# Reciprocal deviations: one pass per group on two tensor operands, or scalar passes per tile, with a new order of issue

## The chip, the cores and the metric

The kernel runs on one core of a Trainium2 chip. The metric is the device time of one execution in microseconds (us); where several executions are told of together, it is their median. The profile and the trace are of one profiled execution of the kernel before.

The engines have short names here. PE multiplies matrices, and PEld is its weight load. DVE works on vectors, ACT applies functions, POOL is a second, slower vector engine, and SP issues the transfers between the memory of the core and the chip's main memory. Each engine takes its instructions in order and waits for the others by semaphores.

## The reference

The input is one array x of 2048 rows and 512 columns. Two kinds of layer alternate, four in all, each fed with a layer norm of x and added back to x:

```python
def _layernorm(x, axis=-1, eps=1e-5):
    m = jnp.mean(x, axis=axis, keepdims=True)
    v = jnp.var(x, axis=axis, keepdims=True)
    return (x - m) / jnp.sqrt(v + eps)
...
X = jnp.fft.rfft2(x) * (w_r + 1j * w_i); y = jnp.fft.irfft2(X)      # A
y = einsum((x @ w_gate) * (x @ w_up), w_down)                       # B, inner width 1792
...
x = x + A(layernorm(x)); x = x + B(layernorm(x))
x = x + A(layernorm(x)); x = x + B(layernorm(x))
```

What matters for the change is the division by the deviation, sqrt(v + eps), once per row and layer.

## The kernel before, in words

x stays in the core as xs, 16 tiles of 128 rows and 512 columns. A spectral layer takes each tile through a forward transform (fwd, line 452, results E), then 16 middle steps that multiply by the filter (middles, tiles fs, dp, zp, vq), then an inverse transform per tile (inv, tiles yi and yo), whose result is added to xs. All transforms are matrix products on PE. The feed-forward follows in blocks of 128 of the 1792 inner columns: up products (gx, gy, gw, gz, gv) from the normalised input, kept as xA and xS, with weights wt; then down products (db, or ex, ey, ez, ev, ew), added to xs by DVE. The products are split in a high and a low part each, and fewer products than the plain count are made by sums beforehand, so that ACT and POOL are busy with rounding, differences and sums.

Layer norm runs tile by tile. `stats` (line 396) puts mean and variance of a tile into mv, by DVE (bn_stats, bn_aggr) or by two passes of ACT (sq) and two small tensor_scalar of DVE. `rstd` (line 412) then works on a group of tiles that share mv and the four-row tile rs. ACT makes a first value of 1/sqrt(v + eps), r, and r²/2. DVE refines it: row 1 is (v + eps) · r²/2; row 2 is (row 1 - 1.5) · r, the negated refined value; for the inverse side, row 3 is -mean · row 2. Each of these is one `scalar_tensor_tensor` over all tiles of the group, with two operands in the core's memory and one constant. Groups hold two tiles, but for the first four forward tiles, which are groups of one. There are 18 forward groups with two passes and 16 inverse ones with three: 84 passes.

Who reads rs: on the forward side, ACT multiplies the tile's transform matrix (tw or tws) by row 2 before PE may use it (fwd_rest, line 459). On the inverse side, `normed` (line 428) lets ACT make xn from xs with row 2 as factor and row 3 as offset; PE then transposes xn into tq (first eight tiles of a layer, build_x), or DVE transposes it and it goes through main memory (last eight, stage_x).

The order of the work is fixed beforehand. The kernel first lists 4811 steps, each with its engine and with what it reads and writes, by keys such as (rs, 2); `Plan.op` (line 231) makes of these which step needs which. ORDER, a packed string, holds the order in which the steps are issued; every engine gets its own in that order. PLACES holds, for each tile that is first used, which buffer of its ring it takes. Both strings were worked out ahead from estimates of each step's time, and the kernel only reads them (`Plan.order`, line 258). In this order, the first eight inverse transforms of a layer precede the feed-forward; the last eight are woven into its first half.

Of the kernel before, what the change touches and what calls it, by code (L numbers as in the profile page):

```python
# [28 lines left out]
def consts():  # L29
# [91 lines left out]
    'CQT5`mje7G9&*SD2dVCFXH)k{30Z8XaKe0qBI%O$i`JswVQmLRiQL44^IBZ{-Uu<xYvO8@;L589YFbgpr8neE+TP^pfm1cs)n-&JbRnPN<IhIQJ`O}u8{6~4c2&)>*Fj2tJkG%cqaCh&ad+Z'
    '$RwQy@-kTE9nRxU{4)*V8T1xxVn1eF=Ln1~MtAu-_rm&<DFgCNq}72o1?#v8#lc#HyW4z$YvZ@Kndc&O*C+Hl!&%I)XfJwKs5-qvUxA+#tW%tC;C@vc%$r#3ybX>+(CSUT=EO#?<18Ay8~yw'
    'Pn}`9Y&2T=IyI|L|{5**+_Ng7M62AeRmZDkKY-@~Kqfj7rl1|^KR*mksmN#=pT$hFQCQv(Az(QCW^N-lE6;*^5S7Kz-px0HVZ=ugWdB4u?3-2qWx-vAA-%zQ>V;#}`E`ES6<4G5se~4Xc1Y+'
    'H2x19##ybbnkNn`j)j9kXz86{0LHKt{*2_4|?Xf@`ofkzp7pT_Zr^bqz5&`10&#xLN9X*8ZRgiln(%<{VXc8bOMd~g#+Ii?Q3taqzmpJbub)aOI|lt!scYRJoR?<L4hcsj=eT)b_{qNAel-h'
    '5chPFN=M=8(<#&%(b#_#k+#O<z(WT{V<?;`>)<-0@MYQ6B3aKwN2v>pHM1kw`fb4fLg@JOdQ<hPT&(%_eah#EXWML633>^tc345J_&KA9yOi5B(YV-q-vB&FAN67T>1LxU<a_HL<R${Q-7W5'
    '$k@!FXQ_&3g@o)ja9ugB#BR3RhEXBrqEDWj)%KLcnbaFB;tz3&T=WkY*>8e4B}=s)*9^U8hLgK*Q_!*iU=gDmIRmbBrj-rR-ZTI-}zU_r5K`5d1I-t*Uz>y?{gCGqFt_t`OUk_wXLN}n0pE_'
    ';1q|O{x~1v?&7<S&2lj&+uaY(jW)7k67KeMeeAuxg|=I+EY6FY<1z#L7N$IxN0(eKML{aUV+g$fZjVxBUd9C!!FQmiFjE4)yPVo%&8hI_1ZoBUji&>yw@KmFyaQ1<k8hajE|o(ONt<G&tFDY'
    'G3y(7Nr|Q<wgAyGBc?AW$z?)&M@?F4^cPs@!<7wo*Oit&j%=D%i0om3=UfYhS7{d7&lddv5;WA<82lzcsC9#IT-Ew?aMYJ2m&r-honLC>EJk(nNzC)oG$!NK*KV2a4wj0=Q2dwBiRxe?;@gQ'
    '1@vB}nezg?iA66LrIjI2x9?m8&0s8r5}<yhp?KaexJ!}hx1>Kvl@%kcl>T$7ud#T<_BOysCB&ev%<6GBa>J2YLC=BhW<5E+;oJkz~l?pME0!`&E;FsJd`g3?@q`4<r`fViHB)o!^})JUm5&k'
    '`m5b?YHF%G`duBxpSgxdrCj<v9Ax6*IZ+6(jL;51--+e1%$K#AW2t%J7BV$TGcQAC8y8FSoc3W~TejOoL3sD%Noae7D2u4PA-}ASdrY1p6KNR1TxEtcJA`$=6*ZZQwFN8Y+T<A6YVTTRhpy$'  # L130
    '&f;VX%7zT(_;67dCW~S3n8}>@Jo-=I04Zt9$Dj0=wcmgxjr4n>^R6>a;MP<cNtkV4biGTY%&EIUUprJnLFX_+u`A2(PeOVgxg>w;x|z*I>XgTWWCn?Ne{Tc&2Ny7$4Q`PIY&az2e=je!tc93'
    'VI>3kluPE`v=XuJ6Ht2r7W5@#)xvEHgt|;_>&O=HIZpLrY!xbvHLe(u#73__Eir{9CwU$1T-d<@isTyZgb7zPRmA0*SheeXc(k9Zj`Cx;UIY63&_#C{vDg8(CE>{ic(sg>tUlL^h9}pe@3}9'
    'y@w~C7oSSIJ^2i`clX0n>i#3xG$u4?=!1nT8$oD7HAM4NakgbfYRT<X1mydh3Y&mz;NRHdj&jjO8I#9+p@X`>B2zSNkFXLlA$>oLI(^llX7kW-ZR^MZWyM100yMv3m89dU~pw*_THyg5OX7e'
    'C(nYmAGvlYGX9kRYxXJCg9v7ZN@8SeQuQVg^f)3eX5cyp)!iG8cMhI;s?o@AE}_G8e;h~<JY|3qe-scYl|?dEumZ3>PRUUhoK&cPVT&D*^%0*728tY{@hJ_jm3^{$yHH{TX0$0M=MUB2Xfr;'
    '<+RulTB0ipZv6bT2Dtx)YG!YxX*S<CU}%sW;CKnVf&aE8tsZWyni+=i7zIF9(1H1|oLN@(R&Z@bH4y!aCUVX>X%V@_N_|MN+$Aak5K_?(DdcX2W*yQ}Ob_9OJS$-@J+aGR;pR{qD}Q!@Wy9)'
    'TVMjpnw4NqtiUi8)ip(V&B!3#!tXUsCvL4FAU#(ZEfU#qv)nMqS|(ro$|P|?%W;pJ*yFRl2?*iAQEo$-m-Dfw^Rxu@c@oq-uJd0u=yC<l-lEYJKCfxij_5nWt`&)o~$v~o@0@H0#y#Vo!{E~'
    ')h^;XW{cO~Bm${j<13IrFPt61s`>EQOcwNR=?$;DnPtj)b79X-y{~LnShYk}KVDd9SaNFuHSjLk5XFc_Ei#Or1lHS&oLog?PMjkB`G{CzDdKf!g0XO%B9@9;4fz@SVT@P@dC1+1kVhCIx`8}'
    'DBted~aDP0HpxN$Un#|WIU@9T@^u_99_$2j&UkL>bS+dppI2KcX@H8F>qBG)nyhgar;G&z#D1aTxXvHG9r+}W|A7QVHVD-IudJwq{;$*7I12_%7<!LQbktS-M9p^I4a^#MF?urqdv78@AZ1('
    'vQR5=P2iy_JHm1rzI&GYFgE`Us=RtnH6pyz3zS}e;TOT0-vfawMO$C$Z5yK{iHEPbo~)dw;egtOy_q+fDX%(%pBsV`99EPh>Wst+&4A=<bIbUFYTE*cfdVmuiPTb?Vv%Qq>JKcJVe)=$&{zF'
    '7n_Z@Y9e3-Y{)yC-=fW;_Qgk5#*$EU^SUcT=sEVyQt-(t4H(X)^D`-FAG8jn<~=IJR&qu6wCurE&-$>%`Io$VH@{hhs77lW^*w5_+0<;?8W09Lu|*mo6F|ccIdW#QKep{jTu0p!Xl8r4xzwG'  # L140
    '~&_Fp4hmc{zdc-kD`Gr6>vTHtoWw*P%OpqSoM*SSUU&vC4R?a#0*}AI`VBA3XSKxfEms&@I0*!rSja1yzwxJk7l@7GmfQlS`VETK<newUPBNY+M*(Cpf$oHyiGY3iy8+?JQnZVg#E+{y91#{'
    'gL*+nrQvOkw;(%*DD~Np@N^^kdIY)f2F8V|r0eoAt%g0G4C^R~)!5Ym3fTe#wT+9Y+`>uLN2QCk93OVpBxnwjYG61h6|LsEaH?g*zT3dt#;62F&}4U$-qQ#&5jzjlTzrCui>L6%kW^>2TU75'
    'Z(X4jWjMRdA+*mVGNB4s~m*Q--VmP7lEOx1`I91SVSEX(<tR#T?AqQGaMjf}0&$$w&17_^gZbLNr`Q}IV^_ZpiM1wb2WS_>8VQxVppP4*2n6udiJxb!2prnrQ<^)_7VCFIQbI(w$bri^Gpk|'
    '3Ns*{O443)WGgQe-XF1n-SEQu~Hsl1D%k4+VLQ$TG`qH;@JPc-#QP>+t2fQI(-QF;wH(9Z{T6=}x1qox)0q9qu$2gf@u6*4~z9Y|bXq*d$*puz3z_h_ufdy9Q?V9Nu5+iECZC$+Y}3W?Qpr;'
    'zb(8L_UXU787nwgT!of-m2tquwRRTX5hzG>zY*8QjUmBJxI{R+Ron6f#Lo`WR0HxvXQOU7l+2aSuC&X`Zi7Q7+2}M%>B5>s>BE3Ch)0#99jp6w>InRVDv0u*wxKrCpJHFWX4{ebh^^A|sLMB'
    'bbqfs=vMZ|NW>(Lm>;tCWtVtRt_?<w`T1C<RiO^m)F9R3a~*#kAcfoKvzaH>^|>pYcz_);%+Y-J+Q(G#Evt31pfFv{O<sMLm*v0x18k7-WHx=!-8m}0`7#+JKl8bBd%EB!u>3jx}f9>TA9jk'
    'KgjlgM1DvoPIHiWUN+*ONLh4qN-aowYgK^q<jxD8=;Jyl+z89aP+p5DrZZF>JJhAp-e2}#<lYFSMfy1LS}C;m&e(9oX9m74Ks6olUlx1_*|vd~Y7@w>62u#-P#td*cDV$cTpT_!(+<g-V(SB'
    'g<syqb2;@EAG;kIgszTCJN(D-(?_J>Q_8`Y#h34KqTNASnawqSG4G(I=!nZVEm>j-NSG|8wvBG*y1y>4{K`!4zsD=cg1|Z|YhzTWCkMTAg)nRvDhgzZxYKNQP<OXbmvEMn+)B?C6U+s|LA=m'
    'jHcar~@|1zOYGXEVu4NV_l|9)}$8Trg;fAoHQYQgqW5KjV>h%>42>j5`3SLy|MN{4hWqQmoag}*^QzYib5n<;!A$Zj*g201jRc^H+5o$kOB?}LTs0OMRY?Vap%m<6RwhDY5{ja^f3P35-1>V'
    '6V3>@c2$t9SWp5|lL^wpt^IyF<Zuw)Prs@GYQ|+S-p5X_e4BCs?q^B5tX@w<=ii8c=vHo}_C(?ZM!9iPGVqp{`2gEG%LLsv4vAnGQeN0K1o7U<_6}p<Uq$peqS+A{iBqbdkdp1N!o96}0<<L'  # L150
    '5a`S@2SB))?k_wy#G`1S2A8BjlE}p|7&V5L;8>9^+`5j=^l85<n`*>JvqP=;iom#Yb7?#K~*WevHd)OhQedkDkYr}Av+<$WFf<ThT|OUW(6d%3w6#Z4ru1_<MDRLWG`xh)f#z6m|d<Lo~_58'
    '9z3uGIF462|Dqgh)zv2hiAjv^NoS}%ed>AuYxM+jiB#)fhPg{1?MV39GM)kidB6?9Gt`#Av-^RL(qJ{)So*+=K}iOzIEBXp%Sn&jV!p(lFCguCRGZfT^Cj~V)nyNj7jtQXdU_^MOT6|{S0W0'
    'D1}XsGJON}=6r80X_DVF0QcbQ#_6kEhs6o3a(+S^CDw4H`H7mqI%@kz(;-)57q704I=c%Gnvlu%c1qR)$*ijI@X!KPcs}+o)57i%+&}+2RbpaKlc}&ng*K@aESK{8M5H$S>Y&nhNOs@7>C2A'
    'Yw58n=}0w*(%hpoS;SyA#ry2kcw?VBd(%KnP+u$Pgvky5cvWz!6?)A4bZyK-%)IS^YFBPe|lAE%e0%Z3zZzST}`3U5~oo9_CP>^~WGbyXwCL)Jg*;!GpV?nZw=j%P3<&NSph(9}3^=l3XDYd'
    '8B-@|?u$Xk^JskTej}f836zx8PNd3tYG<i})i5`U%7jU`$#8c}@bxu1lv-w^(|eXXD$0{!2sS8SE(r$Z?`O*63ds*Q;S`o1N&Onpy6mDbi%S4n```9j=1OP%NAed4@s;*A%g};IecWzd!IY8'
    'tx*D#Mk0lGsP&K^MTeb>RDNE_p^48L%~D9oMVaP@}2K4BPXuacOcRs>%^Z^cRsI`f>iZUT#tT{N|3X)|LVC7>aEQ|&7;6TkF((M0=H4I)l;ZyjCy=7Z^MeB=k@UHv%re&Fe+Vb(r6VP&6!%o'
# [1011 lines left out]
```

## Time and profile before

| what | value |
|---|---|
| median of 3 runs | 1048.07 us (1047.96 to 1051.95) |
| profiled execution | 1046.97 us |
| its span, first to last instruction | 1045.2 us |
| mean granted PE clock | 0.999 |
| busy, DVE / ACT / POOL | 799.7 / 419.4 / 747.8 us |
| main memory traffic | 193.66 MB, 185 GB/s on average |

A row of a group or of the order of time names the engine, the operation, the tiles as out<-in, and shapes as partitions x elements. In rows in order of time, the first number is the start and the second the duration, both in us, and a bracket gives the time that the engine had stood idle and what released it. In a row of a stretch, the numbers after the length are busy time and count for each engine, then the PE clock, the share of the transfer engines and GB/s. All helpers record under line 304 of the kernel, so rows are told apart by their tiles.

The table of stretches, in us from the span's start: forward transforms of the first layer up to about 28, the middle steps to 71, first inverse transforms to about 100, the first feed-forward to 525, in whose second half the forward transforms of the next layer are woven, the last forward transforms to 548, middle steps to 590, inverse transforms to 625, and the second feed-forward to the end.

### The profile page before, as it was taken

What the parts mean: (1) busy time and instruction counts of PE and PEld (TensorE: products, weight loads), DVE (VectorE), ACT (ScalarE), POOL (GpSimd) and SP (SyncE); (2) the same over time, 40 slices, a digit from 0 to 9 for tenths busy, and PEclk for the clock granted to TensorE, in tenths of its full rate; (3) what the DMA queues carried; (4) which work ended last, traced back from release to release, by engine and by line L of the source; (5) the groups of instructions that cost most, each with busy time, mean ns of one, the idle gap of its engine ahead of it and who ended that gap; (6) DMA issues with size and microseconds to landing.
All of it is one profiled execution on the core that took longest, in us unless ns stands there. A gap on an engine that the chain in (4) does not pass through costs nothing.

```text
span 1045.2 us, 18605 instructions
## 1 busy us (share of the span) xinstructions
PE 1023.6 (98%) x6544; PEld 878.4 (84%) x6544; DVE 799.7 (77%) x1457; ACT 419.4 (40%) x989; POOL 747.8 (72%) x950
## 2 busy tenths in 40 slices
PE   8998999999999999999999999999999999999998
PEld 6777987888888888889987779888888888888897
DVE  8779778768866677777878796788897766777778
ACT  6678534423432422232276693322343411222221
POOL 6978999999998665666698467555679954456571
PEclk9999999999999999999999999999999999999999
DMA  9613476586694864665282006446786265565532
GB/s 359 277 66 122 123 261 225 181 276 219 190 293 165 284 212 131 220 209 187 76 302 95 10 3 207 157 140 236 212 254 203 99 216 199 196 217 184 199 122 82
DMA packets 129469, 193.66 MB, mean 185 GB/s; under 512 B 39264, under 2 KB 50784, under 8 KB 127328
## 3 DMA queue, kind: packets, MB, share of 16 engines
q1 hardware_dynamic: 129232, 192.21, 54.3%
q8 instruction: 52, 0.85, 0.3%
q14 instruction: 41, 0.34, 0.1%
q10 hardware_dynamic: 144, 0.26, 0.1%
HBM read 145.52 MB, written 46.92 MB: 184 GB/s over the span
## 4 chain that ended last, share of the span: by engine, by line
PE 89%; DVE 6%; ACT 2%; DMA 2%; issue 1%; DVEq 0%; SPq 0%; ACTq 0%
PE gz L304 15%; PE gx L304 14%; PE db L304 7%; PE gv L304 7%; PE gw L304 7%; PE gy L304 7%; PE ez L304 5%; PE ex L304 5%; PE ev L304 3%; PE zp L304 3%; PE dp L304 3%; PE vq L304 3%; PE ew L304 3%; PE ey L304 2%; DVE xs L304 2%; PE yi L304 2%
## 5 line engine op out<-in xcount | busy, mean ns | idle before, releaser
L304 PE MATMUL gx<-xA,wt 128*128 128x512 f32 (+1 forms) x756 | 175.3, 367 | 1.6 <-DMA wt<-gu 1.6
L304 PEld LDWEIGHTS gx<-xA,wt 128*128 128x128 f32 x756 | 130.6, 189 | 23.6 <-DMA wt<-gu 1.8
L304 POOL TENSOR_TENSOR sf<-q,sf 128x256 fp32r<-128x256 f32 x92 | 68.2, 744 | 78.5 <-ACT sf L304 71.4
L304 POOL TENSOR_TENSOR sf<-cc,sf 128x256 fp32r<-128x256 f32 x96 | 71.3, 745 | 54.9 <-ACT sf L304 54.2
L304 DVE TENSOR_TENSOR xs<-xs,db 128x512 f32<-128x512 f32 x128 | 85.3, 682 | 24.3 <-PE db L304 23.7
L304 PE MATMUL db<-wd,h 128*128 128x512 f32 x336 | 90.6, 392 | 0.7 <-DVE xs L304 0.6
L304 PE MATMUL gz<-xS,wt 128*128 128x512 f32 (+1 forms) x378 | 88.4, 369 | 1.2 <-DVE q L304 1.1
L304 PE MATMUL gy<-xS,wt 128*128 128x512 f32 (+1 forms) x378 | 88.3, 369 | 0.2
L304 PE MATMUL gz<-xA,wt 128*128 128x512 f32 (+1 forms) x378 | 88.1, 368 | 0.0
L304 PE MATMUL gw<-xS,wt 128*128 128x512 f32 (+1 forms) x378 | 87.8, 367 | 0.0
L304 PE MATMUL gv<-xS,wt 128*128 128x512 f32 (+1 forms) x378 | 87.5, 367 | 0.0
L304 PEld LDWEIGHTS gv<-xS,wt 128*128 128x128 f32 x378 | 65.5, 189 | 11.2 <-POOL xS L304 0.2
L304 PEld LDWEIGHTS gz<-xS,wt 128*128 128x128 f32 x378 | 64.5, 189 | 12.0 <-DVE q L304 1.9
L304 ACT COPY s<-gx 128x512 f32<-128x512 f32 (+1 forms) x63 | 33.9, 538 | 101.1 <-PE gx L304 97.5
L304 PEld LDWEIGHTS gw<-xS,wt 128*128 128x128 f32 x378 | 65.2, 189 | 10.9
L304 PEld LDWEIGHTS db<-wd,h 128*128 128x128 f32 x336 | 62.1, 188 | 14.6 <-DVE xs L304 1.7
L304 PEld LDWEIGHTS gy<-xS,wt 128*128 128x128 f32 x378 | 64.5, 189 | 11.2 <-DVE q L304 0.8
L304 PEld LDWEIGHTS gz<-xA,wt 128*128 128x128 f32 x378 | 64.8, 189 | 10.5
L304 ACT CAST sf<-q 128x256 fp32r<-128x256 f32 x92 | 37.1, 406 | 77.8 <-DVE q L304 41.7
L304 DVE TENSOR_TENSOR q<-gy,s 128x512 f32<-128x512 f32 (+1 forms) x63 | 39.6, 628 | 37.5 <-PE gy L304 23.2
L304 POOL TENSOR_TENSOR wt<-rg,wt 128x512 fp32r<-128x512 f32 (+1 forms) x56 | 64.0, 1159 | 3.4 <-ACT wt L304 3.4
L304 ACT CAST sf<-cc 128x256 fp32r<-128x256 f32 x96 | 39.0, 407 | 65.3 <-PE ez L304 16.2
(166 smaller groups left out, 2515.2 us busy)
## 6 DMA issues: line engine op xcount, KB each, us to landing
wt<-gu SPq DMA_DIRECT2D x36, 1024.0 KB, 6.8
wt<-gu SPq DMA_DIRECT2D x36, 768.0 KB, 5.6
bf<-dn SPq DMA_DIRECT2D x20, 1024.0 KB, 5.5
wq<-in_wf_dram SPq DMA_DIRECT2D x16, 1024.0 KB, 11.1
bf<-dn SPq DMA_DIRECT2D x20, 768.0 KB, 4.8
gu<-wt SPq DMA_DIRECT2D x14, 1024.0 KB, 6.4
gu<-wt SPq DMA_DIRECT2D x14, 768.0 KB, 6.0
rg<-in_wb_dram SPq DMA_DIRECT2D x14, 512.0 KB, 4.1
```

Of the source, the lines that this page charges most:

```text
L304: ins = f(*args, **kw)
```

## The change

`rstd` now works tile by tile. Each pass is a `tensor_scalar`: one column of mv or rs is the tensor operand, and the second operand is handed over as a scalar per partition. The formulas stay. ACT's two steps are still made once per group. The keys get the tile's number, so that a reader depends on its own tile's passes alone. Passes go from 84 to 160, steps from 4811 to 4887.

```diff
-        act(130, lambda: A.activation(v()[:, 1, :n], v()[:, 0, :n], AF.Square, scale=0.5 ** 0.5), [(v, 0)], [(v, 1)])
-        c = lambda j: v()[:, j, :n]
-        m = lambda j: mv()[:, :n, j]
-        ops = [(1, EPS, ALU.add, lambda: m(1), lambda: c(1)), (2, -1.5, ALU.add, lambda: c(1), lambda: c(0))]
-        if not fwd:
-            ops.append((3, -1.0, ALU.mult, lambda: m(0), lambda: c(2)))
-        for j, k, op, x, y in ops:
-            dve(10, lambda j=j, k=k, op=op, x=x, y=y: stt(c(j), x(), k, y(), op0=op, op1=ALU.mult),
-                {1: [*mvs, (v, 1)], 2: [(v, 0), (v, 1)], 3: [*mvs, (v, 2)]}[j], [(v, j)])
+        act(130, lambda: A.activation(v()[:, 1, :n], v()[:, 0, :n], AF.Square, scale=0.5 ** 0.5), [(v, 0)], [(v, 1, i) for i in range(n)])
+        ts = V.tensor_scalar
+        for i in range(n):
+            c = lambda j, i=i: v()[:, j, i:i + 1]
+            m = lambda j, i=i: mv()[:, i, j:j + 1]
+            dve(10, lambda c=c, m=m: ts(c(1), m(1), EPS, c(1), op0=ALU.add, op1=ALU.mult), [(mv, i)], [(v, 1, i)])
+            dve(10, lambda c=c: ts(c(2), c(1), -1.5, c(0), op0=ALU.add, op1=ALU.mult), [(v, 0), (v, 1, i)], [(v, 2, i)])
+            if not fwd:
+                dve(10, lambda c=c, m=m: ts(c(3), m(0), -1.0, c(2), op0=ALU.mult, op1=ALU.mult), [(v, 2, i), (mv, i)],
+                    [(v, 3, i)])
...
-            [("xs", t), (nm.v, 2), (nm.v, 3)], [xn], more=0.22)
+            [("xs", t), (nm.v, 2, i), (nm.v, 3, i)], [xn], more=0.22)
...
-        act(128, lambda: A.mul(tw(), tw(), nm.v()[:, 2, i:i + 1]), [(nm.v, 2)], [tw], more=0.13)
+        act(128, lambda: A.mul(tw(), tw(), nm.v()[:, 2, i:i + 1]), [(nm.v, 2, i)], [tw], more=0.13)
```

ORDER and PLACES are replaced as a whole. Unpacked and set against the old order, with the passes on rs left out, 685 of PE's 1052 steps have the same place in PE's own order, 556 of DVE's 1372, 292 of ACT's 960, 176 of POOL's 945 and 61 of SP's 397; on average a step of PE moves by 2 places, of DVE by 6, of ACT, POOL and SP by 4 to 5.

More of the change, by code (lines that the diff above doesn't have):

```diff
@@ L121 @@
[L121 to L156, printed above, removed]
@@ new lines @@
+    'c-l=`2Y3}#)1GtgO%Dkz5a|*+ibyp<igZMpNReW}f_zf^M35>dRT2FJ73?4&iV#phP(Tncbiqc6h#(y)0YV5#_RRmz>?ZzCp1pVP*;A*y^UiFDqNzMZQ68V<+vq%(p|f0)u5m2g#C6UjIzus'
+    '(NQVC8YG}W~<){RmV1t%QxUTaRu8i+%Xi30ajx)Iwe&6IuxX<Gl++V=6V)(p^)^aqJvYF%xEZPgW3dK=1Doy7&9y64{h+SNpLYV0kTg+XKEP7SOo(z?vEBLfnV;QH|G?&H0sVy_lH`81U)un'
+    'j4f%zQHVbM$0Er}7w`C0s0hLL44uR#m5d{?FeTmy4E?7uWcqNOx`W%G3|jybkq4(94q5xc6Q>;BAlWByo3p$5fbrsI4KJ?qkT^t>G_T;lRNe-=m5LF~IcBw)~UKiAjx9h^*`VeNPt4JjvL#S'
+    'pcot1P=@UaRZ1r{$bvpaZNG#&1h|&{lv^W%x4Hp}9N)t#9Mp=XfPQh*>@U6H<$zT%5vEGMV5{WMJqXT)*pGEHqr1e&Xgh+d8fa87{}lX%uVIJz04K`iM@W@Wj$@{3u<7WUg{e8o?9v{066dj'
@@ new lines @@
+    'yKXmoi7J_s)O&^lpgxsv3JA`rEOdfmSLbdS?>d$uBVHq!}xqc_feYu;-ipi9`0vAFTMqppaERK??HmM<J8yr63fXOQEQ$?rLf=U`5jn~fy52X<2P}41{PKV`@CQGGFK%f`jhWi+J}A(agz4D'
+    '4O%mLdU=vUr`hN@hFyw956ABxcqdNN88*SZ3~lA<N3_;bJ2QHv@zeNx4A&(*Igjg3)w9ey*t`$_=!f6CSfu@jn`#DgY2F!X2DM#O30-y<s4477)?LHWcPIPfJE*R9K+gB5loHjxrLDBt$*EM'
+    'Fc0&URXuE^t$$TAcpvQ(-dppZct6|;?cy@(5>a!3e_6>gozsli#u>OZA9jks$W1OXl<{%%z7^fc4m-?y{+F@Vf6P01#&1fjkN83{L5+4{upRn|nS=#{x;#CWgG@WN+#R$3u-#icPdEA4tRol'
+    'b0|8(`nZFqK-k74CD@IC|i@8TSeRJ;8Ot9I4<bofO>d{>9|dvLBIMh~i~GHr`qL-{*8in%vnw@snN2e>~hH=R6pks5Lz^h;ph>a*w=iv(`RZkOua(~xxxP8QZR53$JpaasTm`UUORAfb)e=_'
@@ new lines @@
+    'L@JNs`1Vi5t3u~^kMo~ikm;Ql1t!$g((WcIBur0=yQE>r`$SemN!BdLB}#~SU_qgJWq#^7l`m47mP+S64tf;w1heOJ&|cYA+OzhPbyR6@@3O7$k0!yk7C=J&JGkY+Yg*^3M6d*Zu()oHb^A~'
+    'UsyZpB(#X=dsHmx|HXI(wHQ+gPY9v4>(wIkm2un7caocoTiTPwVcd^nVG&?!|L%2NRD_tB%&}CZq^`T(cK>3vfoYS)dh&EX~yYI_UoaAnl<N')
+PLACES = (
+    '001021000000000000000010122133014430000012004515050000016360078100670171190ab00c11de01f0g010200h02143014560c900fb0e1d02a108001g02h9f00524011'
+    '50b06000c0da2e8960f0h00010121450a00021fd60b120h15000ae021fb00h0c00d120010e0001000712b01089a00fg10hd026c14020230501eb10221f011g2h1d0630010c40'
+    '502010120000421e050b450hd0f0g60100109c4050201e0001gf00164106010bdgf00100he01401025000300bef0h00081b00gd1h3f020700e0d001c22100111001b9h530f01'
+    '0021000c500e3018d001010066207301090200501f27101e017c000016g000211e37009100070g031500001800bf001001g903100001000002eg000009210b0101ea10001510'
+    '1b600ef0903702bg0910e00002a201800100010300b120c0000710010ea3050010010110100261ec073000010000f70014001a5060135bc070610ea10001040000920d101070'
+    'e0100110010010ac5010390101000601041120001700d10020af091030b0600c10103000000000004712f3a0h02g00c041e401050020130f1070g8a0g42610140004030d007f'
+    '014g00602ed10b013221g0003200f0072015640b100700200014020003a100401b507f100800c0201000540300bf041107020308344061520013405011087000060230040810'
+    '412g02000050h70030180023010030c00012314000f120058g0010b300124541f00001201c0010g780b0011023041f1101200000g240h00203400f0310111000b0gh10040238'
+    '040f1312000150014210h000b0410027100c430500210f410h0121613010641003g00211701c072121421811f000003d12201762591011097063g2000058b40cah010e1f0202'
+    'd10197302406001g01c480b2e0000d5h3af0700921004801b060g2000e00acf0021401h06100200702d103010010385b101ce2a0141h028690012030gf17050154230db1c110'
+    '00041ae1320000h0115009120200821320006g71f5c00003d0b10104000ae0h908008057f02g00000120c601d0002b1ah76e34010g03001f0c70000010003e4521ac9a010f83'
+    '0100011c204f127020050003410ab4710030206100e6001402003d0a09g165b00h2161411e000100803220g11071641a52700010f02310043120108b07hd00c5410g21f00314'
+    '24200019000b2078132000a0010340h01170c9200f3000bg005401800eh076b9f06a305e1240gf10600003200144311070012c003061e1010d30800000bg1010h009270124c6'
+    '0e81001f0g01d20000be12401a0001032411h91033207200b0010106c3200f041100805013h091407a10020133100g104130041102400c130b101000650d31240e1001009000'
+    '103g0f0a0000010100023c04251402304h10017b0d0030000a60c01f002311040e10002002h0407001351300000gc020093102e1001004h01003070g510234610e001010000b'
+    'h00244091a10d100g0324000710050b310009600281042403103d410701001b500g0301002c0004126914010001403b1082031120da00ec000901006012g340h10410018031d'
+    '0234100001a010340be6000f00032013042000d180003400he00221501002130710a2000b0g00f1001001210100')
```

80 lines of the change are left out of this document (44 added, 36 removed).

## The prediction

> **What bounds the kernel now.** I read the page first, then stretches of the span, then the instructions on tile rs (the reciprocal deviations), then single stretches in order of time.
>
> ```profile
> span 1045.2 us, 18605 instructions
> PE 1023.6 (98%) x6544; PEld 878.4 (84%) x6544; DVE 799.7 (77%) x1457; ACT 419.4 (40%) x989; POOL 747.8 (72%) x950
> ```
>
> PE is recorded busy for all but 21.6 us of the span. No change off PE can gain more than part of these 21.6 us, about 2%. So the first question is where PE idles. The windows answer it; the first entry after the length is PE's busy time.
>
> ```profile
> 10.00:30.00 20.00, 18.24 (x162) 16.42 (x163) 17.77 (x58) 14.85 (x47) 14.74 (x24) 1.00 1.04 417
> 71.00:100.00 29.00, 25.77 (x165) 19.88 (x164) 25.55 (x73) 23.07 (x66) 24.14 (x32) 1.00 0.34 114
> 100.00:240.00 140.00, 138.30 (x693) 116.83 (x693) 104.95 (x193) 59.74 (x132) 132.00 (x147) 1.00 0.62 210
> 100.00:525.00 425.00, 422.92 (x2285) 365.22 (x2284) 319.86 (x559) 154.61 (x356) 342.21 (x400) 1.00 0.60 201
> 525.00:548.00 23.00, 21.47 (x180) 19.36 (x180) 18.01 (x42) 16.27 (x45) 20.68 (x33) 1.00 0.85 302
> 590.00:625.00 35.00, 32.66 (x227) 26.63 (x226) 29.68 (x85) 28.83 (x78) 21.28 (x31) 1.00 0.03 9
> ```
>
> PE idles 1.8 us in 10 to 30 (first forward transforms), 3.2 us in 71 to 100 (first inverse transforms), 2.1 us in 100 to 525 (first feed-forward), 1.5 us in 525 to 548 and 2.3 us in 590 to 625: together 10.9 us. In the four short stretches DVE is busy 78 to 89% of the time, and every tile passes through its statistics there before PE can use it. So DVE is the engine to read next.
>
> Minimum, median and maximum ns of DVE's passes on rs, and of the one small tensor_scalar that it already runs:
>
> ```profile
> L304 DVE SCALAR_TENSOR_TENSOR rs<-mv,rs x50: 136/280/1217, 6.4 to 770.8; 128x2 f32<-128x2 f32 x46, 128x1 f32<-128x1 f32 x4
> L304 DVE SCALAR_TENSOR_TENSOR rs<-rs x34: 136/337/1232, 7.5 to 767.2; 128x2 f32<-128x2 f32 x30, 128x1 f32<-128x1 f32 x4
> L304 DVE TENSOR_SCALAR mv<-ac x28: 115/144/155, 78.1 to 613.1; 128x1 f32<-128x1 f32 x28
> ```
>
> Work on one or two elements takes between 136 and 1232 ns when two operands come from SBUF, and never over 155 ns when one does. The order of time shows what the long ones wait for:
>
> ```profile
> 80.54 1.42 POOL L304 TENSOR_TENSOR vs<-yc 128x256 f32<-128x256 f32 x2 [0.29 <-ACT yc L304]
> 81.27 0.12 DVE L304 TENSOR_SCALAR mv<-ac 128x1 f32<-128x1 f32 x1
> ...
> 172.75 1.31 POOL L304 TENSOR_TENSOR h<-q,h 128x512 fp32r<-128x512 f32 x1
> 172.84 1.23 DVE L304 SCALAR_TENSOR_TENSOR rs<-rs 128x2 f32<-128x2 f32 x1
> 174.02 1.29 POOL L304 TENSOR_TENSOR u<-rw,u 128x512 fp32r<-128x512 f32 x1
> 174.11 1.22 DVE L304 SCALAR_TENSOR_TENSOR rs<-mv,rs 128x2 f32<-128x2 f32 x1
> 175.36 0.82 ACT L304 ACTIVATE xn<-xs,rs 128x512 f32<-128x512 f32 x1 [3.15 <-DVE rs L304]
> 176.79 0.57 ACT L304 COPY s<-gx 128x512 f32<-128x512 f32 x1
> 177.40 0.69 DVE L304 TENSOR_TENSOR q<-gy,s 128x512 f32<-128x512 f32 x1
> 178.15 1.19 PE L304 MATMUL gz<-xS,wt 128*128 128x512 f32 x4 [1.12 <-DVE q L304]
> ```
>
> POOL's pass ends at 174.06 and DVE's, begun 0.09 us after it, at 174.07; the next pair ends at 175.31 and 175.33. A scalar_tensor_tensor that starts while POOL runs ends when POOL's instruction ends. The tensor_scalar at 81.27 starts inside POOL's second pass and takes 0.12 us. Then the price travels: ACT stood 3.15 us for rs, so s, q and gz came late and PE idled 1.12 us, in the middle of the feed-forward.
>
> **The change part by part.** The passes go from 84 on groups to 160 on single tiles: the eight passes of the four single-tile groups stay as many, the other 76 double. What an unhindered pass costs DVE:
>
> ```profile
> 87.56 0.15 DVE L304 SCALAR_TENSOR_TENSOR rs<-mv,rs 128x2 f32<-128x2 f32 x1
> 87.64 0.41 DVE L304 TENSOR_TENSOR xs<-xs,yo 128x256 f32<-128x256 f32 x1
> ```
>
> It is recorded for 0.15 us, but the next independent instruction begins 0.08 us later, so it occupies 0.08 us of DVE (0.15 where the next reads its result; the new order mostly puts the other tile's pass, or other work, between).
>
> DVE's time on rs in the stretches that matter:
>
> ```profile
> 0.00:28.00 28.00, 6.87 (x20) 1.00 0.94 364
> 71.00:100.00 29.00, 4.31 (x11) 1.00 0.34 114
> 100.00:525.00 425.00, 11.23 (x22) 1.00 0.60 201
> 525.00:548.00 23.00, 3.06 (x8) 1.00 0.85 302
> 590.00:625.00 35.00, 3.99 (x12) 1.00 0.03 9
> ```
>
> No row shows a tensor_scalar with a per-partition operand for its scalar. Its price lies between the 0.12 us of the small tensor_scalar above and 0.40 us, the mean of the 73 records of these rows (29.46 us), if it waited just as long; it can't be below nothing, since an instruction takes its turn. I take the former, since shape, engine and the single tensor operand agree. Of each sum I take 0.08 us a record, for the overlap, and then 0.08 us for each new pass. First stretch: 6.87 - 1.60 - 32 x 0.08 = 2.7 us saved. 71 to 100: 4.31 - 0.88 - 1.76 = 1.7. 100 to 525: 11.23 - 1.76 - 3.52 = 6.0. 525 to 548: 3.06 - 0.64 - 1.28 = 1.1. 590 to 625: 3.99 - 0.96 - 1.92 = 1.1.
>
> What of it reaches the end:
> - First forward transforms: 2.7 us saved, but PE idles only 1.8 us there; beyond that its own transforms are the limit. I take 1.7.
> - First inverse transforms. The first pair's passes lie on the chain of waits:
>
> ```profile
> 82.15 1.05 DVE rs L304
> 83.20 0.33 DVE xs L304
> 83.53 0.89 DVE rs L304
> 84.42 0.07 DVE xs L304
> 84.49 0.18 issue
> 84.67 0.46 DVE rs L304
> 85.14 0.02 issue
> 85.16 1.52 ACT xn L304 x2
> ```
>
>   In the new order two other instructions, a difference from yi and the addition that ends here at 83.53, still stand between the first pass and the last, and I leave the addition where it is; three passes behind it, xn can start near 84.0 instead of 85.16, which is 1.1. DVE's saving is 1.7. I take 1.3 of the 3.2 us idle.
> - 525 to 548: DVE sets the pace at the end of it; I take the 1.1 saved, under the 1.5 idle.
> - 590 to 625: 1.1 saved, 2.3 idle; I take 1.0, as ACT is busy for 28.8 of 35 us and limits the rest.
> - 100 to 525: PE loses 2.1 us in all; the stall quoted above is 1.1 of it. I take 1.2. The other 3.9 us of DVE's saving lie beside PE's work and are worth nothing.
>
> Sum 6.3 us. The profiled execution took 1046.97 us (span 1045.2); the median of the runs is 1048.07, 0.1% more. Against the median: 1048.07 - 6.3 = 1041.8.
>
> The new order of issue: unpacked, it keeps 685 of PE's 1052 steps at their very place. The sequence of PE's work in the four short stretches is the same but for swaps of neighbours; what moves is which of the eight later inverse transforms of a layer comes when, and a shift by one or two of down products against up products. SP's transfers move by 5 places on average. Buffer indices only rename. I cost all this at nothing on average: PE's 422.9 busy us of 425 cover it. If the cover is gone, one wait such as the 1.1 us of gz is the unit of loss, up or down a few of them. POOL gains little: an unhindered pass that came first could hold it up by 0.15 us at most.
>
> **The rivals.**
> *Given back in the feed-forward.* POOL is busy 132.0 of the 140 us after 100. If it can't supply weights and low parts sooner, the 3.0 us of the first two stretches and the 1.2 us there come back as PE waits; the 2.1 us of the second layer stay: 1048.07 - 2.1 = 1046.0. For: POOL's 94%. Against: PE shows no wait for POOL there now, only for DVE.
> *Late passes block ACT.* The new order spreads the passes of the later inverse groups far: in the first of them the second tile's last pass stands some two dozen DVE steps after its first. ACT runs in order; an xn that stands there for its pass holds s behind it, then q, then gz, as at 175.36. Price 1.12 us of PE each; 16 such xn in both layers. Without the 1.2 us of the feed-forward the gain is 5.1 us, so from five stalls on it is slower than before, from ten on by over 0.5%; with twelve it is 1048.07 - 5.1 + 13.4 = 1056.4. Against: in the new order 14 of the 16 xn stand eight or more steps of the whole list behind their last pass, so the pass has time to come first.
> *The passes still wait.* If the scalar form met POOL as the old one does, 160 waits would stand for 84: the 6.3 us would turn round and grow by 76/84 to a loss of 5.7, so 1053.8. The row at 81.27 speaks against it. The Trainium skill (SBUF — State Buffer, "Who interferes with whom") says that a tensor_scalar can run in a two-port mode, and then contends with GpSimd for the whole instruction; by that rule this rival holds. Its condition (VectorE: DVE Perf Modes, "Mode 2×_2P") asks for an outermost non-unit dimension that is even, and a single element has none; the 28 short passes agree with that.
> *More than I count.* All 10.9 us of idle time go: 1037.2.
>
> **How the numbers follow.** Forecast (1039 to 1045) 0.60; given back 0.20; more than counted 0.09; late passes 0.08; still waiting 0.03. A measurement of this kernel tells about 0.5% from no change, so "faster" means under 1042.8: two thirds of the forecast and the fourth rival, 0.50. Slower by over 0.5% is above 1053.3: half of the late passes, the waiting case and a little for the order, 0.09. The rest is 0.41. The range runs from the last rival to past the given-back case, with three stalls of 1.1 us: 1037.2 to 1049.0.
>
> **What would show it.** Passes on rs: 160 tensor_scalar, none over 0.2 us; DVE busy some 10 us less; ACT's wait for rs, 3.15 us at its longest, under 1 us; PE idle in 71 to 100 near 2 us and in 10 to 30 near nothing. I am wrong if passes of 0.3 us and more remain, if PE's idle time turns up between 100 and 525, or if the short stretches keep their length though DVE has less to do.

## The result and the profile after

The changed kernel takes 1037.73 us (median of 4 runs, 1037.49 to 1038.15). Beside it the kernel before took 1048.78 us (4 runs, 1047.96 to 1051.95). The ratio is 0.989, with an interval of 0.9868 to 0.9911: 1.1% faster. The profiled execution took 1037.49 us, 9.5 us less than that of before (1046.97 us, itself 1.8 us under the median of its kernel).

The head of the page after:

```profile
span 1035.7 us, 18681 instructions
PE 1020.6 (99%) x6544; PEld 878.8 (85%) x6544; DVE 793.7 (77%) x1533; ACT 419.7 (41%) x989; POOL 745.8 (72%) x950
```

PE idles 15.1 us of its span, against 21.6 us. That is 6.5 us of the 9.5 us; the other 3.0 us came out of PE's busy time, though it still issues the same 6544 matmuls. The stretches of the prediction, after the change:

```profile
10.00:30.00 20.00, 18.31 (x179) 17.03 (x179) 16.66 (x64) 14.46 (x44) 16.35 (x27) 1.00 1.03 402
71.00:100.00 29.00, 26.99 (x180) 21.43 (x180) 26.93 (x90) 25.65 (x71) 25.40 (x33) 1.00 0.03 10
100.00:240.00 140.00, 140.00 (x694) 118.73 (x693) 103.80 (x201) 57.92 (x127) 133.82 (x148) 1.00 0.69 233
100.00:525.00 425.00, 424.66 (x2310) 368.69 (x2309) 318.21 (x587) 157.92 (x366) 345.84 (x406) 1.00 0.64 212
525.00:548.00 23.00, 21.58 (x216) 18.22 (x216) 14.76 (x40) 15.53 (x37) 21.91 (x36) 1.00 0.85 334
590.00:625.00 35.00, 33.41 (x248) 29.03 (x247) 32.00 (x105) 29.82 (x83) 24.54 (x35) 1.00 0.14 43
```

PE never idles in 100 to 240 any more. In 100 to 525 its idle time falls by 1.7 us only (2.1 to 0.3), but it completes 2310 matmuls where it completed 2285. The count says more than the busy time; the section on the prediction comes back to it.

The passes on rs after the change, beside the small tensor_scalar that stood there before:

```profile
L303 DVE TENSOR_SCALAR rs<-mv,rs x96: 172/205/215, 6.2 to 763.8; 128x1 f32<-128x1 f32 x96
L303 DVE TENSOR_SCALAR rs<-rs x64: 171/205/215, 6.4 to 759.9; 128x1 f32<-128x1 f32 x64
L303 DVE TENSOR_SCALAR mv<-ac x28: 122/146/154, 78.0 to 605.4; 128x1 f32<-128x1 f32 x28
```

None of the 160 is recorded for more than 215 ns; the longest of the 84 took 1232. Of the 84, 46 took over 250 ns, and every one of these ended 13 to 20 ns after an instruction of POOL. Of the 160, 88 end while an instruction of POOL still has more than 50 ns to run. In order of time, amid a long instruction of POOL:

```profile
80.58 1.28 POOL L303 TENSOR_TENSOR wt<-rg,wt 128x512 fp32r<-128x512 f32 x1
80.97 0.33 DVE L303 TENSOR_SCALAR rs<-mv,rs 128x1 f32<-128x1 f32 x2
81.21 0.21 DVE L303 TENSOR_SCALAR rs<-rs 128x1 f32<-128x1 f32 x1
```

Three passes begin and end within POOL's 1.28 us. What waits for the passes now: ACT's xn before stood idle for rs 9 times, 14.3 us in all; after:

```profile
ACT xn L303 <- DVE rs L303: 8.0, 4, 4.0
```

That is 4 times, 8.0 us, 4.0 at the longest. It did not become short, only rarer, and in the first feed-forward PE is hardly ever idle behind it.

To see where the time went, four points in PE's work serve as milestones, read from its groups on dp, gx, tp and tq (first and last start):

```profile
L303 PE MATMUL dp<-df,fs x512: 272/273/328, 26.8 to 573.6; 128*64 128x128 f32 x171
L303 PE MATMUL gx<-xA,wt x756: 277/390/505, 91.7 to 1025.7; 128*128 128x512 f32 x147, 128*128 128x256 f32 x42
L303 PE MATMUL tp<-tw,fo x128: 270/276/276, 432.9 to 536.7; 128*128 128x128 f32 x128
L303 PE MATMUL tq<-ident,xn x64: 270/273/330, 82.8 to 613.1; 128*128 128x128 f32 x64
```

The first dp ends the first layer's forward transforms, the first gx the middle steps and the first inverse transforms, the last tp the first feed-forward with the next layer's forward transforms, the last dp the middle steps, the last tq the inverse transforms, the last gx nearly the whole. The lengths between them, in us, read in the same way for each kernel of the next section:

| kernel | to first dp | to first gx | to last tp | to last dp | to last tq | to last gx | last gx at |
|---|---|---|---|---|---|---|---|
| before | 28.2 | 66.1 | 449.8 | 36.8 | 40.5 | 414.3 | 1035.7 |
| after | 26.8 | 64.9 | 445.0 | 36.9 | 39.5 | 412.6 | 1025.7 |
| after, a second time (e10) | 26.9 | 64.9 | 444.8 | 36.9 | 39.5 | 412.4 | 1025.4 |
| new passes alone (e1) | 26.7 | 65.4 | 446.2 | 36.8 | 39.9 | 414.1 | 1029.1 |
| new order alone (e2) | 29.2 | 66.3 | 452.7 | 36.8 | 40.9 | 412.8 | 1038.7 |
| two operands per tile (e3) | 31.3 | 67.5 | 453.9 | 36.9 | 41.3 | 413.5 | 1044.4 |
| new passes, woven groups (e4) | 28.3 | 66.2 | 446.6 | 36.8 | 40.6 | 414.3 | 1032.8 |
| new passes, other groups (e5) | 26.5 | 65.4 | 449.7 | 36.8 | 39.9 | 414.3 | 1032.6 |
| passes 2 and 3 twice (e6) | 29.6 | 68.3 | 449.4 | 36.9 | 42.9 | 414.7 | 1041.8 |
| old order, then new (e8) | 26.5 | 65.4 | 447.4 | 36.8 | 39.5 | 412.4 | 1028.0 |
| new order, then old (e11) | 26.6 | 64.9 | 445.7 | 36.8 | 39.9 | 414.1 | 1028.0 |
| old order longer, then new (e12) | 26.3 | 65.4 | 445.4 | 36.8 | 41.4 | 412.4 | 1027.7 |
| two elements (e9) | 27.3 | 66.1 | 445.6 | 36.8 | 40.1 | 412.3 | 1028.2 |

Two executions of the changed kernel agree within 0.2 us in every length, so tenths can be read here, with care between kernels whose buffers are numbered otherwise (e12 and e1 run the same steps up to the last tp and differ by 0.8 us in the column "to last tp"). Behind the last gx, which the lengths leave out, lie 9.5 us before and 10.0 us after; that is why the last column shows a gain of 10.0 us and the span one of 9.5.

### The profile page after: what moved, and what is told of

It is laid out like the page before. It is cut to its first block, busy times and chain, and to the rows that moved or that the text cites. A ratio compares the mean times of both kernels' runs of the same rounds, so it can differ in the third digit from the quotient of the medians.

```text
span 1035.7 us, 18681 instructions
## 1 busy us (share of the span) xinstructions
PE 1020.6 (99%) x6544; PEld 878.8 (85%) x6544; DVE 793.7 (77%) x1533; ACT 419.7 (41%) x989; POOL 745.8 (72%) x950
## 4 chain that ended last, share of the span: by engine, by line
PE 93%; DVE 4%; DMA 1%; ACT 1%; issue 1%; POOL 1%; SPq 0%; DVEq 0%; ACTq 0%
PE gz L303 15%; PE gx L303 15%; PE db L303 8%; PE gw L303 7%; PE gy L303 7%; PE gv L303 7%; PE ex L303 5%; PE ez L303 5%; PE ew L303 3%; PE dp L303 3%; PE zp L303 3%; PE ev L303 3%; PE vq L303 3%; PE ey L303 3%; PE tp L303 3%; DVE xs L303 2%
## 5 line engine op out<-in xcount | busy, mean ns | idle before, releaser
L303 POOL TENSOR_TENSOR sf<-q,sf 128x256 fp32r<-128x256 f32 x99 | 73.2, 744 | 84.4 <-ACT sf L303 79.9
L303 ACT CAST sf<-q 128x256 fp32r<-128x256 f32 x99 | 39.9, 406 | 101.5 <-DVE q L303 53.7
L303 PEld LDWEIGHTS gw<-xS,wt 128*128 128x128 f32 x378 | 65.4, 189 | 10.9
L303 PEld LDWEIGHTS ez<-bf,sf 128*128 128x128 f32 x402 | 56.3, 190 | 5.2 <-issue 0.7
```

What stands on the lines that cost most here:

```text
L303: ins = f(*args, **kw)
```

## The experiments

**The passes alone and the order alone.** e1 has the new passes in the order and the buffers of before, each pass of a group replaced in place by those of its tiles. In words, against the changed kernel:

```text
-ORDER, PLACES: those of the changed kernel
+ORDER, PLACES: those of before, a group's pass replaced by its tiles' passes
```

> The 160 scalar passes per tile, but everything else in the old order with the old buffer indices: where a group's pass stood, its tiles' passes stand one behind the other. My theory (the two-operand passes wait for POOL, and that wait is what cost) expects most of the 10 to 11 us: 1038 to 1042. The rival that the gain lies in the new order expects 1046 to 1050, no different from before.

Measured 1040.01 us (1039.46 to 1040.49), ratio 0.9912 (0.9893 to 0.9932). e2 has the new order, and in it the 84 passes of before (shortened):

```diff
-ops per tile: V.tensor_scalar(c(1), m(1), EPS, c(1), ...) and so on
+ops per group: stt(c(j), x(), k, y(), op0=op, op1=ALU.mult)
```

> The new order and indices, with the old group passes on two operands (84, each at the place where the first tile's pass now stands). My theory expects the waits back and a time within 4 us of before: 1044 to 1052. The rival that the order gives the gain expects 1037 to 1041.

Measured 1050.24 us (1049.34 to 1050.69), ratio 1.0008 (0.9997 to 1.002). So the new order alone gives no gain that shows (its median lies 1.7 us above that of before, within the scatter of before), the new passes alone 8 to 9 us, and both together 2.3 to 2.8 us more than the passes alone. In e2 the waits for POOL are all there:

```profile
L300 DVE SCALAR_TENSOR_TENSOR rs<-mv,rs x50: 144/370/1628, 6.4 to 774.4; 128x2 f32<-128x2 f32 x46, 128x1 f32<-128x1 f32 x4
```

**Is it the form, or the single tile?** e3 is the changed kernel, order and 160 passes, with each pass as a scalar_tensor_tensor on its one element (one of three passes is shown, the call written out):

```diff
-ts(c(1), m(1), EPS, c(1), op0=ALU.add, op1=ALU.mult)
+stt(c(1), m(1), EPS, c(1), op0=ALU.add, op1=ALU.mult)
```

> As after in order, count and tile keys (160 passes of one element per partition), but each pass is a scalar_tensor_tensor with two operands in SBUF. My theory expects each to wait for POOL's running instruction, a mean of 0.35 to 0.40 us and a maximum over 1.1 us, and a time of 1046 to 1056. The rival that the gain comes from letting each tile go on by itself, whatever the passes cost, expects 1037 to 1040.

Measured 1056.26 us (1055.12 to 1057.66), ratio 1.0069 (1.005 to 1.0087), a little over the upper end.

```profile
L301 DVE SCALAR_TENSOR_TENSOR rs<-mv,rs x96: 130/160/1201, 6.3 to 782.3; 128x1 f32<-128x1 f32 x96
L301 DVE SCALAR_TENSOR_TENSOR rs<-rs x64: 120/159/1199, 7.0 to 778.5; 128x1 f32<-128x1 f32 x64
```

The median pass is shorter than the new form's (160 against 205 ns). What costs is the tail up to 1.2 us: 63 records are over 250 ns, and each of them ends 13 to 21 ns after an instruction of POOL. The mean, 0.354 us, is the expected one. The same element, the same order and one changed form: 18.5 us between e3 and the changed kernel. (In e3's profile PE was granted half its clock for 3.4 us among the first inverse transforms; half of 3.4 us, 1.7 us, is an estimate of the most that this costs.) On one element, the form is what counts. Nor does the gain come from letting each tile go on by itself, since e3 does that as well.

**What a pass costs when nothing hinders it.** e6 issues passes 2 and 3 twice, 96 more instructions that write the same values again (pass 2 is shown, pass 3 is doubled in the same way):

```diff
-dve(10, lambda c=c: ts(c(2), c(1), -1.5, c(0), ...), ...)
+for _ in range(2):
+    dve(10, lambda c=c: ts(c(2), c(1), -1.5, c(0), ...), ...)
```

> As after, with each second and third pass issued twice in a row (same operands and result): 96 more passes of about 0.2 us, 64 of them on the inverse side. If DVE sets the pace in the short stretches, their 60 or so extra passes cost 2 to 5 us: 1040 to 1043. If DVE has room there now, and the chain is elsewhere, at most 1 us: 1037.5 to 1038.7.

Measured 1053.68 us (1052.28 to 1055.1), ratio 1.0046 (1.003 to 1.0062). Both expectations were far too low: 16 us more than the changed kernel, 0.17 us for each extra pass. In order of time, first the changed kernel, then e6:

```profile
6.44 0.21 DVE L303 TENSOR_SCALAR rs<-rs 128x1 f32<-128x1 f32 x1
6.57 0.68 DVE L303 BATCH_NORM_STATS2 st<-xs 128x6 f32<-128x512 f32 x1
```

```profile
6.40 0.46 DVE L302 TENSOR_SCALAR rs<-rs 128x1 f32<-128x1 f32 x2
6.78 0.69 DVE L302 BATCH_NORM_STATS2 st<-xs 128x6 f32<-128x512 f32 x1
```

One pass holds up the next instruction by 0.13 us, two by 0.38: the repeat, which touches the element just written, takes 0.25 us of DVE. So e6 doubles something dearer than an unhindered pass. All 96 repeats start 0.21 to 0.25 us after the pass before them, and the changed kernel has the same interval, 0.24 to 0.25 us, in the 14 places where a pass stands right behind the one whose result it reads; elsewhere the next instruction, if it needn't wait, starts 0.12 to 0.13 us after a pass in most cases. 96 times 0.25 are 24 us, of which 16 reach the end. By the table they do so everywhere: 2.8 us in the first forward transforms, 3.4 in the first inverse ones (where PE was also granted half its clock for 6.8 us), 4.4 in the column "to last tp", 3.4 and 2.1 in the second layer. By the starts of the same matmuls, 2.8 of the 4.4 us come before 520 us, in the feed-forward itself. So added time on DVE reaches PE also in the stretch where the prediction wrote 3.9 us of DVE's time off as lying beside PE's work.

**Where the passes gain.** e4 and e5 divide e1: the order of before, and the new form only in the 12 woven groups that are issued within the feed-forwards (e4), or only in the other 22 (e5).

```diff
+NEW = (14, 15, 16, 17, 18, 19, 20, 21, 30, 31, 32, 33)
+count["g"] = count.get("g", -1) + 1
+if count["g"] in NEW:
...
+else:
+    for j, k, op, x, y in ops:
+        dve(10, lambda j=j, k=k, op=op, x=x, y=y: stt(c(j), x(), k, y(), op0=op, op1=ALU.mult), ...)
```

> Old order. Scalar passes only in the 12 groups that are woven into the feed-forwards (eight later inverse groups, four forward groups of the second layer's first half); the other 22 keep the two-operand group passes. The new passes alone gave 8.5 us. If the waits inside the feed-forward were worth the 1.2 us of the prediction: 1046 to 1048. If more of the gain lies there, as the milestones of that run suggest (2 to 4 us): 1043.5 to 1046.

> Old order. Scalar passes only in the 22 groups of the four short stretches, where PE waits for DVE; the 12 woven groups keep the old passes. By the prediction's sum (5.1 of 6.3 us) this has most of the gain: 1041 to 1044. If the woven groups have half of it: 1044 to 1046.

Measured: e4 1044.03 us (1043.5 to 1050.74, 12 runs), ratio 0.9966 (0.9947 to 0.9985); e5 1044.16 us (1042.9 to 1048.4, 9 runs), ratio 0.9958 (0.994 to 0.9976); before, on the same chip, 1048.03. By these medians the woven groups give 4.0 us (1.6 to 5.6 by the interval), where the prediction had 1.2, the others 3.9 (2.5 to 6.3), where it had 5.1. So e4 fell into its second range, e5 to the border of its two. Their sum, 7.9 us, is near the 8.5 of e1. By the table e4 gains 3.2 us between the first gx and the last tp, 2.9 up to the last gx, and nothing in the second feed-forward, where four of its groups lie.

A step-by-step comparison of PE's starts in e4 and before (the same order) shows where. The first place is the stall that the prediction quoted. PE before, without the row of 178.15, which the prediction shows:

```profile
176.19 0.84 PE L304 MATMUL db<-wd,h 128*128 128x512 f32 x3
...
179.73 0.94 PE L304 MATMUL db<-wd,h 128*128 128x512 f32 x3
180.50 1.54 PE L304 MATMUL gv<-xS,wt 128*128 128x512 f32 x6
181.89 1.52 PE L304 MATMUL db<-wd,h 128*128 128x512 f32 x6
```

and the same work in e4, under DVE's passes and ACT's xn there:

```profile
172.67 0.30 DVE L304 TENSOR_SCALAR rs<-mv,rs 128x1 f32<-128x1 f32 x2
172.89 0.33 DVE L304 TENSOR_SCALAR rs<-rs 128x1 f32<-128x1 f32 x2
173.13 0.33 DVE L304 TENSOR_SCALAR rs<-mv,rs 128x1 f32<-128x1 f32 x2
173.50 0.82 ACT L304 ACTIVATE xn<-xs,rs 128x512 f32<-128x512 f32 x1 [1.17 <-DVE rs L304]
176.31 0.84 PE L304 MATMUL db<-wd,h 128*128 128x512 f32 x3
176.99 1.52 PE L304 MATMUL gz<-xS,wt 128*128 128x512 f32 x6
178.35 0.84 PE L304 MATMUL db<-wd,h 128*128 128x512 f32 x3
179.03 1.52 PE L304 MATMUL gv<-xS,wt 128*128 128x512 f32 x6
180.39 1.52 PE L304 MATMUL db<-wd,h 128*128 128x512 f32 x6
```

Six passes end within 0.8 us, where before the two quoted ones alone took 2.5; xn starts at 173.50 instead of 175.36; PE doesn't stop. From the db at 176.19 to that at 181.89 PE needed 5.70 us, in e4 4.08: 1.62 us gained where the trace records 1.12 us of idle time. The difference can be read from the rows. Six matmuls are recorded as 1.52 us, but the next group starts 1.36 us after them, so a record outlasts its matmul's place by 0.16 us, and that much of any gap looks busy. And after the gap PE starts slower: gz to db takes 1.58 us instead of 1.36, db to gv 0.77 instead of 0.68.

The second place is a smaller stall of the same kind, which the prediction did not price. Before:

```profile
222.21 1.07 DVE L304 SCALAR_TENSOR_TENSOR rs<-mv,rs 128x2 f32<-128x2 f32 x1
223.19 1.47 DVE L304 TENSOR_TENSOR xs<-xs,db 128x512 f32<-128x512 f32 x2
```

```profile
222.49 0.85 PE L304 MATMUL db<-wd,h 128*128 128x512 f32 x3
223.92 0.96 PE L304 MATMUL db<-wd,h 128*128 128x512 f32 x3 [0.58 <-DVE xs L304]
224.72 1.53 PE L304 MATMUL gy<-xS,wt 128*128 128x512 f32 x6
```

Again a long pass on two elements stands before the addition for which PE waits. These six db take 2.23 us from the first start to gy; in e4 1.51. That is 0.72 us gained for 0.58 recorded. The remaining 0.9 us of the 3.2 are slips of one or two tenths, with 0.09 us of idle time recorded at the largest. The stretch's rows in e4 and e5:

```profile
100.00:525.00 425.00, 424.73 (x2311) 368.68 (x2310) 317.53 (x583) 157.25 (x363) 344.62 (x404) 1.00 0.61 204
```

```profile
100.00:525.00 425.00, 422.18 (x2278) 364.32 (x2277) 319.85 (x554) 153.16 (x355) 341.93 (x400) 1.00 0.60 203
```

e4 completes 2311 matmuls there, before 2285, and e5, which keeps the two-operand passes in these groups, only 2278. e5 enters the stretch 2.3 us ahead of before and is 1.4 us ahead at its end. It lost 0.9 us, because the same two-operand passes now meet other instructions of POOL:

```profile
269.93 0.74 DVE L303 SCALAR_TENSOR_TENSOR rs<-mv,rs 128x2 f32<-128x2 f32 x1
272.76 1.66 PE L303 MATMUL gy<-xS,wt 128*128 128x512 f32 x6 [0.76 <-DVE q L303]
```

The same pass took 0.15 us before, and gy waited 0.09 us. The table hides what follows: in the last forward transforms, 525 to 548, e5 gains 1.0 us, and e1 does too. Before, the last pair's passes (0.66 and 0.65 us) held up ACT, and PE behind it:

```profile
541.83 0.40 ACT L304 ACTIVATE tw<-tw,rs 128x128 f32<-128x128 f32 x1 [0.94 <-DVE rs L304]
542.28 2.05 PE L304 MATMUL tp<-tw,fo 128*128 128x128 f32 x16 [0.48 <-ACT tw L304]
```

In e5 the four passes in their place take 0.58 us together, and PE doesn't stop for tp. In the column "to last tp" this gain and the loss before it cancel.

**What the order gains.** e8 runs the order of before up to the last forward transforms of the second layer and the new order from there, e11 the reverse, e12 changes to the new one later, among the second layer's inverse transforms. All have the new passes; 14 buffers in e8, 19 in e11 and some in e12 had to be numbered anew for the seams. e10 is the changed kernel again. In words:

```text
-ORDER: the new order
+ORDER (e8): old up to step 2612 of 4887, new from there
+ORDER (e11): new up to step 2685, old from there
+ORDER (e12): old up to step 3020, new from there
```

> All scalar passes; old order up to the last forward transforms of the second layer, new order from there (14 transform buffers renumbered). The new order was worth 2.3 us with these passes. If that lies in the second layer, above all in the wait of gx for the transfer of wt that the old order has at 850 us: 1037.3 to 1038.7. If it lies in the first layer: 1039.3 to 1040.3.

> The changed kernel once more, beside the others on one chip: 1037.2 to 1038.2, the yardstick for the run that mixes the orders.

> All scalar passes; new order up to the last forward transforms of the second layer, old order from there (19 transform buffers renumbered): the counterpart of the run before. If the new order gains about 1 us in the first layer and 1.5 us by sparing the second feed-forward its wait for wt: 1038.5 to 1039.6, and the wait is back. If all of its 2.3 to 2.8 us lie in the first layer: 1037 to 1038.

> All scalar passes; old order up to the second layer's first inverse transforms, some 60 us later than in the run that began the new order at the last forward transforms, new order from there. If the second feed-forward's wait for wt is the order's gain there, and the earlier mixture lost it at its seam: 1038 to 1039. If not: 1039.5 to 1041.

Measured: e8 1040.5 us (1040.07 to 1041.38), ratio 0.992 (0.9899 to 0.9942); e10 1037.2 (1036.83 to 1038.83), 0.9893 (0.9869 to 0.9917); e11 1039.14 (1038.39 to 1039.5), 0.9909 (0.9887 to 0.9931); e12 1040.42 (1039.55 to 1040.65), 0.992 (0.99 to 0.994). e8 lies above both of its ranges, e12 in its second one, e11 in its first, with the wait for wt back as expected; e10 repeats the changed kernel, at the lower end of its range. As totals these don't add up: behind the new first part (e11) the new second part is worth 1.9 us (e10), behind the old one (e8, e12 against e1) nothing.

The table shows most of where it goes. In the second feed-forward, its last column but one, every kernel with the new order there takes 412.3 to 413.5 us (e6 with its extra passes aside), every one with the old order 414.1 to 414.3. About 1.7 us are gained there in e8 and e12 as well. Both lose most of them again at their own seams: e8 takes 447.4 to the last tp (e1 446.2), e12 41.4 in the inverse transforms (e1 39.9), where tq waits 1.5 us for xA. And behind the last gx the new order takes 10.0 to 10.2 us, the old one 9.6 in e1. What is gained in the second feed-forward is one wait of PE for a transfer of weights, seen in e1:

```profile
852.76 1.66 PE L303 MATMUL gx<-xA,wt 128*128 128x512 f32 x6 [1.44 <-DMA wt<-gu]
```

It is 1.6 us before, 1.4 in e1, 1.2 in e11, and absent in after, e8, e10 and e12. The rest of the order's gain lies in the first layer: after against e1, 0.5 us in the inverse transforms and 1.2 in the column "to last tp" (only 0.4 against e12, which runs the same steps as e1 there), and 0.4 in the second layer's inverse transforms. And e2's profile shows why the order alone gives nothing: with the old passes it takes the same second feed-forward down by 1.5 us, but loses 1.0 in the first forward transforms and 2.9 up to the last tp, against the one profile of before.

**Is it the single element?** The prediction's third rival rested on whether a tensor_scalar meets POOL. In e9, the changed kernel's two small tensor_scalar on mv become one on two elements:

```diff
-V.tensor_scalar(nm.mv()[:, i, 0:1], a()[:, 0:1], 1.0 / 512, None, op0=ALU.mult)
-V.tensor_scalar(nm.mv()[:, i, 1:2], a()[:, 2:3], 1.0 / 512, None, op0=ALU.mult)
+V.tensor_scalar(nm.mv()[:, i], a()[:, 0:3:2], 1.0 / 512, None, op0=ALU.mult)
```

> As after, but the two small tensor_scalar that scale ACT's sums into mean and variance become one on two elements per partition (14 for 28), one SBUF operand and an immediate. The theory that an operation with one SBUF operand never waits for POOL expects 0.12 to 0.2 us each and 1036.5 to 1038. The rival, a two-port mode for an even number of elements, expects it to wait like the old passes, with a maximum over 0.6 us, and a time of 1037.5 to 1041.

Measured 1040.36 us (1039.6 to 1041.98), ratio 0.9923 (0.9902 to 0.9943): 14 instructions fewer, and 2.6 to 3.2 us slower than the changed kernel.

```profile
L301 DVE TENSOR_SCALAR mv<-ac x14: 139/461/1068, 78.8 to 607.9; 128x2 f32<-128x2 f32 x14
```

```profile
81.08 1.27 POOL L301 TENSOR_TENSOR wt<-rg,wt 128x512 fp32r<-128x512 f32 x1
81.31 1.07 DVE L301 TENSOR_SCALAR mv<-ac 128x2 f32<-128x2 f32 x1
```

POOL's instruction ends at 82.35, DVE's at 82.38. Of the 14, 8 took over 250 ns, and all 8 ended 24 to 28 ns after an instruction of POOL. On two elements the tensor_scalar waits as the two-operand form did; on one it doesn't. The Trainium skill (SBUF — State Buffer, "Who interferes with whom") says that a tensor_scalar in a two-port mode contends with GpSimd. For that mode the Trainium skill (VectorE: DVE Perf Modes, "Mode 2×_2P") asks that the outermost dimension of more than one element be even, or odd and equal for source and destination. That two elements meet this agrees with the 8 long records. That one element, which has no such dimension, stays outside the mode is an inference, which the 28 short records of the changed kernel bear out.

## Why the prediction was right, and where it was not

It forecast 1041.8 us, in 1037.2 to 1049.0, from a gain of 6.3 us. The profiles show 9.5, the medians 11. The measured 1037.73 us is inside the range, but 0.5 us from its lower end, and below the 1039 to 1045 that the forecast itself covered. By the table, step by step:

| stretch | predicted | after | e1, the passes alone |
|---|---|---|---|
| first forward transforms | 1.7 | 1.4 | 1.5 |
| first inverse transforms | 1.3 | 1.2 | 0.7 |
| first feed-forward and last forward transforms | 1.2 + 1.1 | 4.8 | 3.6 (2.6 + 1.0) |
| second inverse transforms | 1.0 | 1.0 | 0.6 |
| second feed-forward | 0 | 1.7 | 0.2 |

The 2.6 and 1.0 are read from the starts of the same matmuls in e1 and before, which issue their matmuls in the same order; the changed kernel has another.

**The mechanism** was right. Passes with two operands wait till POOL's instruction ends, single-element passes with one don't: e3 puts the waits back by the form alone, e9, in the two small tensor_scalar of the statistics, by a second element.

**The price of a pass** was too low: 0.12 us recorded became 0.205, 0.08 us occupied became 0.12 to 0.13. The row that the price was taken from has a constant as its scalar. In the changed kernel such an instruction is recorded for 0.146 us, and the next one starts 0.06 to 0.07 us after it in 17 of the 22 places where it needn't wait; the scalar per partition doubles that. "None over 0.2 us" failed by that, and so did "DVE busy some 10 us less": it is 6.0. With 0.12 the prediction's own line for the first stretch reads 6.87 - 1.60 - 32 x 0.12 = 1.4 us, which is what came, but by luck: the lines for 525 to 548 and 590 to 625 would read 0.5 and 0.2 us, where e1 shows 1.0 and 0.6.

**The mis-sized term** is the feed-forward: 1.2 us, capped by PE's 2.1 us of idle time, with the other 3.9 us of DVE's saving "beside PE's work and worth nothing". (The 3.9 are the 6.0 saved less the whole 2.1 idle, though only 1.2 were taken.) The passes gained 2.6 us there in e1's profile and 3.1 in e4's. The cap was no cap: PE's records stretch over part of a gap, and work after a gap runs slower, so that 1.12 us recorded were 1.62 lost. The sentence at the start, "no change off PE can gain more than part of these 21.6 us", counts by the same measure. The 9.5 us stay under it, but only 6.5 of them are idle time that went. The Trainium skill (Perfetto Trace Analysis, "Identifying the Most-Contended Engine") calls matmul busy time a poor measure of how near a kernel is to its limit, since matmuls are pipelined. The 25 more matmuls in 100 to 525 for 1.7 us more busy time, and the same 6544 in 3.0 us less, agree.

**The 525 to 548 term**, 1.1 us, came as predicted and where: 1.0 us in e5, which has the new passes there, and in e1. In e5 the wait of ACT for these passes and that of PE for ACT are gone.

**The new order at nothing** was wrong by 2.3 to 2.8 us. It was argued from the busy time of the first feed-forward and from the four short stretches; the second feed-forward was left out, though PE's largest wait for a transfer stood there, 1.6 us at wt<-gu. With the old passes the order shows no gain (e2), so what it is worth depends on the passes that it orders. All three errors, the feed-forward, the order and the price of a pass, are in size; the first two made the gain too small, the third made it too large. That 1037.73 still fell into the range is owed to the width of the range.

**What would show it.** 71 to 100 now has 2.0 us of PE idle, as forecast. 10 to 30 has 1.7, not "near nothing". It is two waits, neither of them for DVE:

```profile
12.06 1.16 PE L303 MATMUL tp<-tws,fo 128*128 128x128 f32 x8 [0.90 <-POOL fo L303]
...
25.80 1.10 PE L303 MATMUL wp<-midt 128*128 128x512 f32 x2 [0.79 <-ACT E L303]
```

ACT's longest wait for rs rose from 3.15 to 4.0 us instead of falling under 1:

```profile
276.14 0.82 ACT L303 ACTIVATE xn<-xs,rs 128x512 f32<-128x512 f32 x1 [3.98 <-DVE rs L303]
```

PE has no idle time at all around it, so this was the wrong sign to look for. None of the three signs of being wrong came: no pass is over 0.215 us, PE's idle time between 100 and 525 went down, and the short stretches became shorter.

**The rivals.** Given back in the feed-forward: POOL is busy 133.8 of 140 us after 100, and PE idles not at all there, so no. Late passes block ACT: the long xn waits exist (4.0 us), but PE doesn't wait behind them. The passes still wait: not on one element; e3 is this rival's case, with 1056.3 us where the prediction priced it at 1053.8. "More than I count", all 10.9 us of idle time for 1037.2, hit the time, but not by its way: the stretches still idle, and the rest came from lost time that no idle row shows and from the second feed-forward.
